# Fetching expert tiles by a plain transfer instead of a row-by-row gather, and a second weight copy on VectorE

## The chip, the core and the metric

The kernel runs on one core of a Trainium2 chip. The metric is device time in microseconds (us). The engines are named as in the profile: PE (TensorE, its weight loads apart as PEld), DVE (VectorE), ACT (ScalarE), POOL (GpSimd) and SP (SyncE, which here only issues transfers). The kernel before was timed three times: 283.83 us median, 283.54 to 286.17.

## The reference

The input passes through an attention block and then through a mixture of experts with one expert per token.

```
phi(x)  = outer product of (S1 x) and (S2 x), 8 x 8 = 64 features       x: 4 batches, 4 heads, 1088 rows, 32 wide
kv      = sum over rows of phi(k) v ;   z = sum over rows of phi(k)
attn    = phi(q) kv / (phi(q) z + 1e-6)                                  -> x: 4352 tokens x 128
logits  = x @ w_gate ;  expert = argmax ;  gate = softmax(logits)[expert]
out[t]  = gate * relu(x[t] @ w1[expert]) @ w2[expert]                    8 experts, w1 128 x 1024, w2 1024 x 128
```

All of it is in fp32.

## The kernel before

**Attention.** Tasks named T, P, V, E, B, U, N (transposes, projections, sums, queries) work on 512-row chunks of each batch. **Routing.** For each batch `b`, C.b chooses the expert, G.b takes the exponentials, R.b ranks the tokens within their experts, and S.b scatters the batch's rows into `xs_dram`, a DRAM table with 4352 places for each expert. A row is 130 words: 128 of x, the gate and the token number. S.b is 8 or 9 indirect transfers on POOL, one for each 128 tokens. So the rows of one expert stand one behind another.

**Tiles.** The expert part works on tiles of 128 rows of one expert: 34 fixed ones (`JMIN`) and up to 7 more, of which parts of 4, 2 and 1 are taken by three branches, as the routing needs them. Tiles 0 to 9 (`JE` is 10) hold rows of batches 0 and 1 alone and may begin before batches 2 and 3 are scattered; tile 10 and later ones wait for all. Two tables, made on VectorE by `table` (tasks W.0 to W.6, and later `piece`), say for each tile which expert it has (`woff`) and where its rows are.

**One tile.** `gather(j)` (task F.j) fetches the tile's rows from `xs_dram` into `xg_of(j)`; `x_in(j)` (I.j) transposes them on PE, copies the transpose on ACT, and lets VectorE copy the expert's w1 (128 x 1024) out of `w1_all` at a register's offset; `up(j)` (Y.j) is 8 matmuls into `ph` and a relu, on ACT for the early tiles and half on ACT, half on VectorE from tile 7 on; `rows_out(j)` makes the numbers of the output rows; `down(j)` (Z.j with `rows_out`) is 8 matmuls into `py` and the scaling by the gate on ACT; `store(j)` scatters the rows to `out` on POOL. In the profile each fp32 matmul stands as two records, so a tile has 16 records of `ph`, 16 of `py` and one transpose `xgTp`.

**Order.** Each engine runs its instructions in the order in which the program records them. ORDER, a list of task names, sets it up to tile 4's `down`; behind it a loop over the tiles takes over: in turn j it records x_in(j+2), rows_out(j), up(j+1), down(j), the gather of tile j+6 (from j = 6 on), a gather of one of the 7 possible extra tiles (`optional`) and the stores.

**What the change touches.** `gather` (L691) is an indirect transfer on POOL with one row number for each partition; `down` (L733) loads a register on PE and addresses `w2_all` with it, so each of its 8 matmuls has a register operation ahead of it; the loop at L842 says how many stores each turn records; `table` (L534) makes the row numbers `grow`.

Of the kernel before, what the change touches and what calls it, by code (L numbers as in the profile page):

```python
# [47 lines left out]
ORDER = """  # L50
finish_s T.K00 T.K01 P.K00 P.K01 T.K11 T.K10 T.kr0 V.K00 P.kr0 D P.K11 P.K10 T.Q00 T.Q01 L T.Q11
V.K01 P.Q01 E.0 P.Q00 B.0 P.Q11 T.qr0 U.Q01 U.Q00 T.K21 T.Q10 N.Q00 P.qr0 N.Q01 C.0 P.Q10 P.K21
V.K10 V.K11 T.kr1 G.0 T.K20 R.0 U.qr0 U.Q11 E.1 P.K20 B.1 A.2 U.Q10 T.Q20 N.qr0 N.Q10 N.Q11 V.K20
V.K21 C.1 P.Q20 P.kr1 G.1 T.K31 T.Q21 A.3 R.1 T.K30 W.0 U.Q20 P.Q21 P.K30 P.K31 E.2 W.1 T.Q30 W.2
T.Q31 T.qr1 W.3 U.Q21 S.0 P.Q31 B.2 W.4 P.Q30 V.K30 S.1 N.Q21 N.Q20 V.K31 P.qr1 W.5 F.0 W.6 E.3 C.2
U.Q30 B.3 F.1 F.2 U.qr1 U.Q31 F.3 N.qr1 F.4 N.Q30 G.2 I.0 F.5 N.Q31 I.1 R.2 Y.0 I.2 I.3 C.3 Y.1 Z.0
I.4 Y.2 Z.1 F.6 G.3 S.2a I.5 S.2b R.3 Y.3 Y.4 S.3a S.3b Z.2 F.7 Y.5 Z.3 F.8 Z.4 I.6 F.9
"""
# [3 lines left out]
def kernel(  # L62
# [111 lines left out]

    zeros = const.tile([128, 128], FP, name="zeros")
    nc.vector.memset(zeros, 0.0)
    idle = bank_ps("idle")
    for i in range(12):
        nc.tensor.matmul(idle[:, 0:128], lhsT=zeros, rhs=zeros, start=True, stop=True)  # L179

# [270 lines left out]

    xs_dram = dram.tile([E * NTOK, XW], I32, name="xs_dram")

    def route(b):
# [74 lines left out]


    tiles = {}
    done = const.tile([128, E], FP, name="done")

    def table(g, n, j0):  # L534
# [30 lines left out]
        if g:  # L565

            bits = const.tile([128, 3], I32, name="bits")
            nc.vector.tensor_scalar(bits[:, 0:1], cum[:, E - 1:E], float(JE - JMIN), None, ALU.add)
            begin = t1("begin", I32)
            for i, (run, below) in enumerate(((4, 0), (2, 4), (1, 6))):  # L570
                if i:
                    nc.vector.tensor_scalar(begin[:, i:i + 1], bits[:, 0:1], below, None, ALU.bitwise_and)
# [219 lines left out]
    for j in range(sum(name[0] == "Z" for name in begun), JMIN):  # L794
# [81 lines left out]
```

## Time and profile before

| | us |
|---|---|
| median of three runs | 283.83 |
| the profiled execution | 284.85 |
| its span, first to last instruction | 282.7 |
| PE busy | 231.8 (82% of the span) |
| DVE / ACT / POOL busy | 108.5 / 75.4 / 134.2 |
| transfers: gathers x41, scatters x34, stores x34 and x7 on POOL | mean 1.05, 1.07, 1.03 and 1.17 each |

A row of the page or of an answer gives an engine's busy time, the idle time ahead of a group and in `<-` what ended it. "issue" is idle time in which the engine waited for nothing that the profile shows. PEclk is TensorE's granted clock as a share of 2.4 GHz (0.5 is 1.2 GHz).

### The profile page before, as it was taken

Reading aid. Unit: us, or ns where it says so; the run is one execution under the profiler, and the core shown is the slowest. Engines: PE = TensorE matmul, PEld = TensorE weight load, DVE = VectorE, ACT = ScalarE, POOL = GpSimd, SP = SyncE. Lnnn points to the kernel's source line nnn. Section 1 sums busy time; section 2 is a strip of 40 time slices with the busy share of each in tenths; the row PEclk is TensorE's granted clock in tenths of the full one; section 3 lists DMA queues with packets and bytes.
Section 4 is the critical chain, followed back from the end, with each engine's and each line's share of the span. In section 5 each row is a group of like instructions: output and inputs, shape, how many; then the busy total and the mean of one; then the engine's idle time right before and its main releaser. Section 6 shows DMA issues by size and latency. Waiting matters only on the chain.

```text
span 282.7 us, 6720 instructions
## 1 busy us (share of the span) xinstructions
PE 231.8 (82%) x2558; PEld 216.2 (76%) x2558; DVE 108.5 (38%) x303; ACT 75.4 (27%) x198; POOL 134.2 (47%) x165
## 2 busy tenths in 40 slices
PE   8989875957975959669939559887887999999993
PEld 7989764836954949539939349787777998999993
DVE  4656735515844805410641012324323234224320
ACT  2555420404340305013200012221212232333321
POOL 5520373273072564740057747667576156263223
PEclk9999997975996886957977758999997999999999
DMA  6969999211011010110002111111110001010000
GB/s 196 286 191 361 367 377 376 84 47 31 2 40 28 30 48 20 59 38 0 2 21 56 36 38 33 50 35 44 33 48 26 17 21 44 14 37 21 20 9 21
DMA packets 23009, 22.69 MB, mean 80 GB/s; under 512 B 5844, under 2 KB 20184, under 8 KB 22976
## 3 DMA queue, kind: packets, MB, share of 16 engines
q1 hardware_dynamic: 18160, 14.95, 16.3%
q0 software_dynamic: 3712, 7.15, 8.6%
q8 instruction: 23, 0.38, 0.6%
q10 hardware_dynamic: 1104, 0.13, 0.3%
q14 instruction: 10, 0.08, 0.1%
HBM read 17.81 MB, written 4.95 MB: 81 GB/s over the span
## 4 chain that ended last, share of the span: by engine, by line
PE 65%; issue 19%; another core or an unknown queue 6%; ACT 3%; DMA 2%; POOL 2%; DVE 1%; POOLq 1%; ACTq 0%; DVEq 0%
PE ph L724 23%; PE py L740 18%; PE kv L342 4%; PE ab_K L319 4%; PE qp_Q L405 3%; PE nd_Q L417 3%; PE ab_Q L319 3%; PE idle L179 2%; PE tp_Q L310 1%; PE xgTp L703 1%; DMA out_dram<-y,to 1%; PE tp_K L310 1%; ACT q_pT_Q L408 1%; POOL out_dram L747 1%
## 5 line engine op out<-in xcount | busy, mean ns | idle before, releaser
L740 PE MATMUL py<-w_all,hT 128*128 x592 | 81.5, 290 | 9.9 <-issue 6.7
L724 PE MATMUL ph<-xgT,w 128*128 128x128 f32 x592 | 83.6, 295 | 7.3 <-issue 5.2
L724 PEld LDWEIGHTS ph<-xgT,w 128*128 128x128 f32 x592 | 77.7, 209 | 12.1 <-issue 9.9
L740 PEld LDWEIGHTS py<-w_all,hT 128*128 128x128 f32 x592 | 75.9, 205 | 12.8 <-issue 10.1
L692 POOL DMA_INDIRECT x_rows<-xs_dram,grow x41 | 42.9, 1047 | 48.4 <-issue 28.2
L731 DVE TENSOR_SCALAR hT<-ph 128x512 f32<-128x512 f32 x30 | 20.7, 691 | 101.6 <-ACT hT L726 70.0
L747 POOL DMA_INDIRECT out_dram<-y,to x34 | 35.0, 1031 | 43.3 <-ACT xgT L705 28.4
L515 POOL DMA_INDIRECT xs_dram<-x_rows,row_i x34 | 36.3, 1067 | 31.9 <-DVE base_e L509 9.5
L726 ACT ACTIVATE hT<-ph 128x512 f32<-128x512 f32 x37 | 22.2, 599 | 73.2 <-PE ph L724 36.9
L709 DVE COPY w<-w_all 128x1024 f32 x38 | 26.4, 704 | 20.7 <-remote 16.6
L743 ACT ACTIVATE y<-py,x_rows 128x128 f32<-128x128 f32 x34 | 12.5, 368 | 60.3 <-remote 27.6
L417 PE MATMUL nd_Q<-kvx,q_pT_Q 128*64 128x82 f32 x256 | 13.0, 244 | 7.0 <-issue 5.7
L703 PE MATMUL xgTp<-ident,x_rows 128*128 128x128 f32 x38 | 10.5, 298 | 7.8 <-DMA x_rows<-xs_dram,grow 4.4
L417 PEld LDWEIGHTS nd_Q<-kvx,q_pT_Q 128*64 128x64 f32 x256 | 10.8, 141 | 7.6 <-issue 5.6
L319 PE MATMUL ab_K<-s_cat,xT_K 128*64 128x64 f32 x256 | 12.0, 233 | 4.8 <-issue 4.4
L327 DVE TENSOR_TENSOR k_p<-half_K 128x1024 f32<-128x1024 f32 x8 | 10.5, 1328 | 11.7 <-issue 6.1
L319 PEld LDWEIGHTS ab_K<-s_cat,xT_K 128*64 128x64 f32 x256 | 9.7, 144 | 6.7 <-issue 6.3
L705 ACT COPY xgT<-xgTp 128x128 f32<-128x128 f32 x38 | 9.5, 265 | 15.3 <-remote 8.0
L327 DVE TENSOR_TENSOR q_p_Q<-half_Q 128x1024 f32<-128x1024 f32 x8 | 10.4, 1324 | 8.1 <-ACT half_Q L326 8.1
L342 PEld LDWEIGHTS kv<-k_p,v_aug 128*33 128x33 f32 x256 | 9.0, 125 | 4.1 <-issue 4.1
L342 PE MATMUL kv<-k_p,v_aug 128*33 128x64 f32 x256 | 10.4, 239 | 1.9 <-issue 1.9
L703 PEld LDWEIGHTS xgTp<-ident,x_rows 128*128 128x128 f32 x38 | 5.5, 149 | 7.5 <-issue 7.2
(164 smaller groups left out, 193.4 us busy)
## 6 DMA issues: line engine op xcount, KB each, us to landing
w_all<-in_moe_w_dram SPq DMA_DIRECT2D x16, 512.0 KB
k<-in_k_dram SPq DMA_DIRECT2D x4, 512.0 KB
v<-in_v_dram SPq DMA_DIRECT2D x4, 512.0 KB
q<-in_q_dram SPq DMA_DIRECT2D x4, 512.0 KB
x_rows<-xs_dram,grow POOLq DMA_INDIRECT x41
xs_dram<-x_rows,row_i POOLq DMA_INDIRECT x34
out_dram<-y,to POOLq DMA_INDIRECT x34
q_rem<-in_q_dram SPq DMA_DIRECT2D x4, 32.0 KB
```

The costliest lines, as they stand in the source:

```text
L319: nc.tensor.matmul(ab[ts(m, 64)].rearrange("p (g i r) -> p g i r", g=4, i=n)[:, :, i], lhsT=st["xT"][:, ds(i * 128 + m * 64, 64)], rhs=s_c ...
L327: nc.vector.tensor_tensor(f.rearrange("p g (a b) -> p g a b", a=R), half[:, :, 0:R, None].broadcast_to(shape), half[:, :, None, R:2 * R].b ...
L342: nc.tensor.matmul(kv[b][g * RR:g * RR + DA, ts(n, RR)], lhsT=v1[:, h], rhs=k_p[:, h], start=(first and n == 0), stop=last, skip_group_che ...
L417: nc.tensor.matmul(nd[ts(m, 64), i, ds(hp * 2 * KC, 2 * KC)], lhsT=t[:, ds((i * NP + hp) * 128 + m * 64, 64)], rhs=kvx[bs[m]][:, hp].rearr ...
L515: d = nc.gpsimd.indirect_dma_start(out=xs_dram[:], out_offset=bass.IndirectOffsetOnAxis(ap=row_i[:, u:u + 1], axis=0), in_=x[:, u, :].bitc ...
L692: d = nc.gpsimd.indirect_dma_start(out=xg_of(j).bitcast(I32), out_offset=None, in_=xs_dram[:], in_offset=bass.IndirectOffsetOnAxis(ap=tile ...
L709: nc.vector.tensor_copy(out=w1, in_=w1_all[:, ds(wo, F)])
L724: nc.tensor.matmul(ph[:, ts(c, 128)], lhsT=w1[:, ts(c, 128)], rhs=xT, start=True, stop=True)
L726: nc.scalar.activation(hT[:, 0:512], ph[:, 0:512], AF.Relu)
L731: nc.vector.tensor_scalar(hT[:, 512:1024], ph[:, 512:1024], 0.0, None, ALU.max)
L740: nc.tensor.matmul(py[:, :DM], lhsT=hT[:, ts(c, 128)], rhs=w2_all[:, ds(wo + c * DM, DM)], start=(c == 0), stop=(c == NFC - 1))
L747: d = nc.gpsimd.indirect_dma_start(out=out[:], out_offset=bass.IndirectOffsetOnAxis(ap=to_of(j), axis=0), in_=y, in_offset=None, bounds_ch ...
```

## The change

Rows come by one plain transfer. `xs_dram` is filled with zeros early, by one transfer on SP's queue between the loads (8 x 128 rows, from a zeroed tile). The tables give each tile's first row instead of 128 row numbers; for a tile that would run past its expert's rows, the first row moves back, and rows that belong to another tile get an output row number outside `out`. `gather` loads that first row into a register of SP and issues a plain 128 x 130 transfer on SP's queue. `up(j)` first copies the expert's w2 on VectorE at a register's offset into one of three buffers (`w2_of`), and `down(j)` reads it there with fixed addresses. Stores are recorded two for each turn of the loop. ORDER is another list.

```
 ORDER = """
-finish_s T.K00 T.K01 P.K00 P.K01 T.K11 T.K10 T.kr0 V.K00 P.kr0 D P.K11 P.K10 T.Q00 T.Q01 L T.Q11
+finish_s T.K00 T.K01 P.K00 P.K01 T.kr0 T.K11 T.K10 P.kr0 D V.K00 P.K10 P.K11 T.Q01 T.Q00 L T.Q11 V.K01 P.Q00
...
-I.4 Y.2 Z.1 F.6 G.3 S.2a I.5 S.2b R.3 Y.3 Y.4 S.3a S.3b Z.2 F.7 Y.5 Z.3 F.8 Z.4 I.6 F.9
+N.Q31 I.1 F.4 R.2 F.5 S.2a Y.0 I.2 S.2b F.6 F.7 N.qr1 C.3 I.3 Y.1 G.3 Z.0 Y.2 I.4 Y.3 Z.1 Y.4 R.3 F.8 Z.2
+S.3a I.5 Z.3 Z.4 W.6 S.3b Y.5 F.9 I.6
...
+    xs_dram = dram.tile([E * NTOK, XW], I32, name="xs_dram")
+    zeros = const.tile([128, XW], FP, name="zeros")
+    nc.vector.memset(zeros, 0.0)
...
     load_rem(lambda b: q_rem[:, b // 2], q, nc.sync, 0)
+    nc.sync.dma_start(out=xs_dram.rearrange("(e r) c -> r e c", e=E)[0:128],
+                      in_=zeros[:, None, :].bitcast(I32).broadcast_to([128, E, XW]))
     load_main("k", k, 2)
...
-        nc.vector.tensor_scalar(loc, loc, 128.0, iota_p, ALU.mult, ALU.add)
+        nc.vector.tensor_scalar(loc, loc, 128.0, None, ALU.mult)
...
+            nc.vector.scalar_tensor_tensor(begin, of, -128.0, loc, ALU.add, ALU.min)
+            nc.vector.tensor_scalar(begin, begin, 0.0, None, ALU.max)
+            nc.vector.scalar_tensor_tensor(first, ej, float(NTOK), begin, ALU.mult, ALU.add)
...
+    def w2_of(j):
+        if not w2_own:
+            w2_own.append([att.tile([128, JC * H, RR], FP, tag="k_p", name=f"w2_0_{i}", bufs=3)
+                           .rearrange("p g f -> p (g f)") for i in range(3)])
+            w2_own.append([])
+        if j >= JMIN and not w2_own[1]:
+            w2_own[1].extend(att.tile([128, F], FP, tag="q_pT", name=f"w2_1_{i}", bufs=3) for i in range(3))
+        return w2_own[j >= JMIN][j % 3]
...
     def gather(j):
-        d = nc.gpsimd.indirect_dma_start(
-            out=xg_of(j).bitcast(I32), out_offset=None, in_=xs_dram[:],
-            in_offset=bass.IndirectOffsetOnAxis(ap=tiles[j][1], axis=0),
-            bounds_check=E * NTOK - 1, oob_is_err=False)
+        _, (row,) = nc.values_load_multi_w_load_instructions(
+            tiles[j][1], engines=[mybir.EngineType.SP], min_val=0, max_val=E * NTOK - 128,
+            skip_runtime_bounds_check_because="the table keeps a tile within its expert's rows")
+        d = nc.sync.dma_start(out=xg_of(j).bitcast(I32), in_=xs_dram[ds(row, 128), :])
...
     def up(j):
         xT, w1 = xT_of(j), w1_of(j)
+        _, (wo,) = nc.values_load_multi_w_load_instructions(
+            tiles[j][0], engines=[DVE], min_val=0, max_val=(E - 1) * F,
+            skip_runtime_bounds_check_because="the table clamps the expert to the last one")
+        nc.vector.tensor_copy(out=w2_of(j), in_=w2_all[:, ds(wo, F)])
...
     def down(j):
-        hT = hT_of(j)
-        _, (wo,) = nc.values_load_multi_w_load_instructions(
-            tiles[j][0], engines=[PE], min_val=0, max_val=(E - 1) * F,
-            skip_runtime_bounds_check_because="the table clamps the expert to the last one")
+        hT, w2 = hT_of(j), w2_of(j)
...
-            nc.tensor.matmul(py[:, :DM], lhsT=hT[:, ts(c, 128)], rhs=w2_all[:, ds(wo + c * DM, DM)],
+            nc.tensor.matmul(py[:, :DM], lhsT=hT[:, ts(c, 128)], rhs=w2[:, ts(c, DM)],
...
-        for _ in range(0 if j < 6 else j % 2 if optional else 2 if j + 1 < JMIN else JT):
+        for _ in range(2 if j + 1 < JMIN else JT):
```

The order on POOL, from the last batch's scatter on; `x_rows` stands for the gathered rows, `out_dram` for the output. Before:

```order
L515 DMA xs_dram<-x_rows_201,row_i_1660 34816x130 x9
L692 DMA x_rows_193<-xs_dram,grow_1314 128x130
L692 DMA x_rows_195<-xs_dram,grow_1314 128x130 x2
L692 DMA x_rows_193<-xs_dram,grow_1870 128x130 x4
L692 DMA x_rows_195<-xs_dram,grow_1870 128x130
L747 DMA out_dram<-y_1571,to_0_1542 4352x128
L692 DMA x_rows_193<-xs_dram,grow_1870 128x130
L692 DMA x_rows_195<-xs_dram,grow_1870 128x130
```

With the change:

```order
L517 DMA xs_dram<-x_rows_195,row_i_754 34816x130 x8
L517 DMA xs_dram<-x_rows_197,row_i_999 34816x130 x9
L517 DMA xs_dram<-x_rows_201,row_i_1476 34816x130 x8
L517 DMA xs_dram<-x_rows_203,row_i_1699 34816x130 x9
L769 DMA out_dram<-y_1615,to_0_1589 4352x128
L769 DMA out_dram<-y_1615,to_1_1590 4352x128
L769 DMA out_dram<-y_1615,to_2_1591 4352x128
```

All gathers have left POOL: the four scatters stand behind one another, and the stores follow at once.

The order on SP, behind the last load of the experts' matrices (`w_all`), where before nothing but the end of the program stood. With the change:

```order
L713 TENSOR_LOAD first_row_1294
L716 ISA
L716 DMA x_rows_195<-xs_dram 128x130
L713 TENSOR_LOAD first_row_1294
L716 ISA
L716 DMA x_rows_195<-xs_dram 128x130
```

Each gather is now a register load, an address operation and one transfer, and these three are repeated for every tile.

The order on VectorE for one of the late tiles: `w` and `w_0_1` are the copies' targets, `to` the output rows, `hT` the relu's half. Before:

```order
L706 TENSOR_LOAD woff_1831
L709 ISA
L709 COPY w_0_1431<-w_all 128x1024
L718 TENSOR_TENSOR to_13_1555<-x_rows_193,inv_i_1890 128x1
L731 TENSOR_SCALAR hT_2_1502<-ph_2176 128x512
```

With the change:

```order
L727 TENSOR_LOAD woff_1861
L730 ISA
L730 COPY w_0_1418<-w_all 128x1024
L739 TENSOR_TENSOR to_13_1603<-x_rows_195,inv_i_1933 128x1
L743 TENSOR_LOAD woff_1861
L746 ISA
L746 COPY w_0_2_1500<-w_all 128x1024
L756 TENSOR_SCALAR hT_2_1513<-ph_2263 128x512
```

A second register load and a second 128 x 1024 copy now stand ahead of the relu of the same turn.

## Rows read from the trace of the kernel before

**Rows 1.** The page's chain that ended last: share of the span by engine.

```profile
PE 65%; issue 19%; another core or an unknown queue 6%; ACT 3%; DMA 2%; POOL 2%; DVE 1%; POOLq 1%; ACTq 0%; DVEq 0%
```

**Rows 2.** Busy time by stretch: each engine's us (instructions), PEclk, DMA share, GB/s.

```profile
20.00:30.00 10.00, 9.98 (x246) 9.41 (x243) 7.46 (x18) 4.62 (x11) 0.60 (x1) 1.00 0.99 334
78.30:90.70 12.40, 7.25 (x97) 5.52 (x94) 4.79 (x19) 3.30 (x10) 7.01 (x7) 0.84 0.15 39
90.70:109.00 18.30, 15.28 (x109) 14.70 (x110) 8.93 (x32) 4.67 (x13) 8.34 (x8) 0.78 0.09 30
109.00:129.40 20.40, 14.68 (x86) 12.66 (x85) 6.31 (x27) 4.49 (x11) 12.13 (x12) 0.75 0.13 40
145.70:216.90 71.20, 57.63 (x400) 53.82 (x401) 18.35 (x44) 13.21 (x37) 48.59 (x47) 0.84 0.14 40
216.90:278.40 61.50, 60.77 (x543) 60.39 (x541) 19.98 (x43) 17.89 (x48) 24.38 (x23) 1.00 0.08 23
```

**Rows 3.** Groups by line, PE: the first of 145.7:216.9, the others of 216.9:278.4.

```profile
L724 PE MATMUL ph<-xgT,w 128*128 128x128 f32 x193 | 30.5, 302 | 6.6 <-issue 5.2 <-ACT xgT L705 0.8
...
L740 PE MATMUL py<-w_all,hT 128*128 x273 | 33.4, 275 | 0.7 <-ACT y L743 0.7
L724 PE MATMUL ph<-xgT,w 128*128 128x128 f32 x256 | 31.2, 275 | 0.0
```

**Rows 4.** Timeline of PE, steady: start us, us, operation, count [idle before <-releaser].

```profile
261.78 0.27 PE L703 MATMUL xgTp<-ident,x_rows 128*128 128x128 f32 x1
...
265.46 0.27 PE L703 MATMUL xgTp<-ident,x_rows 128*128 128x128 f32 x1
```

**Rows 5.** Timeline of PE from the first late tile on.

```profile
145.76 0.45 PE L703 MATMUL xgTp<-ident,x_rows 128*128 128x128 f32 x1 [4.37 <-DMA x_rows<-xs_dram,grow]
146.00 3.63 PE L724 MATMUL ph<-xgT,w 128*128 128x128 f32 x16
149.43 2.99 PE L740 MATMUL py<-w_all,hT 128*128 x16
...
165.11 1.80 PE L724 MATMUL ph<-xgT,w 128*128 128x128 f32 x4 [0.84 <-issue]
...
195.54 0.30 PE L703 MATMUL xgTp<-ident,x_rows 128*128 128x128 f32 x1 [1.81 <-DMA out_dram<-y,to]
```

**Rows 6.** Timeline of POOL: first and last of 18 transfers in a row.

```profile
142.97 1.11 POOL L692 DMA_INDIRECT x_rows<-xs_dram,grow  x1 [18.47 <-issue]
...
165.41 0.99 POOL L692 DMA_INDIRECT x_rows<-xs_dram,grow  x1 [0.30 <-issue]
```

**Rows 7.** Timeline of PE about the first tile.

```profile
81.44 1.36 PE L417 MATMUL nd_Q<-kvx,q_pT_Q 128*64 128x82 f32 x32 [0.73 <-ACT q_pT_Q L408]
...
82.99 0.60 PE L417 MATMUL nd_Q<-kvx,q_pT_Q 128*64 128x82 f32 x7
...
88.39 1.10 PE L417 MATMUL nd_Q<-kvx,q_pT_Q 128*64 128x82 f32 x12 [0.89 <-issue]
...
90.73 3.37 PE L724 MATMUL ph<-xgT,w 128*128 128x128 f32 x16 [0.52 <-DVE den_Q L422]
```

**Rows 8.** The page's groups: busy us, mean ns of one | idle before, releaser.

```profile
L747 POOL DMA_INDIRECT out_dram<-y,to x34 | 35.0, 1031 | 43.3 <-ACT xgT L705 28.4
...
L709 DVE COPY w<-w_all 128x1024 f32 x38 | 26.4, 704 | 20.7 <-remote 16.6
```

**Rows 9.** Timeline of VectorE: two of the w1 copies.

```profile
109.58 0.92 DVE L709 COPY w<-w_all 128x1024 f32 x1 [0.42 <-PE ph L724]
...
142.52 0.69 DVE L709 COPY w<-w_all 128x1024 f32 x1 [0.29 <-issue]
```

**Rows 10.** Timeline of SP's queue: the longest and the last issue of a load.

```profile
22.64 3.80 SPq L150 DMA_DIRECT2D w_all<-in_moe_w_dram  x1
...
44.95 0.43 SPq L151 DMA_DIRECT2D w_all<-in_moe_w_dram  x1
```

**Rows 11.** The chain of waits in order of time: a late gather until it landed.

```profile
142.97 2.65 DMA x_rows<-xs_dram,grow
```

More of the change, by code (lines that the diff above doesn't have):

```diff
@@ L50 @@
 ORDER = """
-finish_s T.K00 T.K01 P.K00 P.K01 T.K11 T.K10 T.kr0 V.K00 P.kr0 D P.K11 P.K10 T.Q00 T.Q01 L T.Q11
[L52 to L56, printed above, removed]
-I.4 Y.2 Z.1 F.6 G.3 S.2a I.5 S.2b R.3 Y.3 Y.4 S.3a S.3b Z.2 F.7 Y.5 Z.3 F.8 Z.4 I.6 F.9
+finish_s T.K00 T.K01 P.K00 P.K01 T.kr0 T.K11 T.K10 P.kr0 D V.K00 P.K10 P.K11 T.Q01 T.Q00 L T.Q11 V.K01 P.Q00
+E.0 P.Q01 B.0 P.Q11 T.qr0 U.Q00 U.Q01 T.Q10 T.K21 N.Q00 P.qr0 P.Q10 N.Q01 V.K10 C.0 P.K21 G.0 V.K11 U.Q10
+T.K20 T.kr1 R.0 U.Q11 E.1 P.K20 U.qr0 B.1 T.Q20 N.qr0 A.3 N.Q11 N.Q10 C.1 A.2 P.Q20 P.kr1 G.1 V.K20 T.K31
+S.0 T.K30 T.Q21 R.1 W.0 V.K21 U.Q20 P.K31 E.2 P.Q21 W.1 P.K30 B.2 T.Q31 W.2 S.1 W.3 T.Q30 U.Q21 T.qr1 N.Q20
+N.Q21 V.K30 P.qr1 W.4 P.Q30 V.K31 W.5 P.Q31 F.0 E.3 U.qr1 U.Q30 B.3 F.1 F.2 F.3 C.2 G.2 U.Q31 N.Q30 I.0
+N.Q31 I.1 F.4 R.2 F.5 S.2a Y.0 I.2 S.2b F.6 F.7 N.qr1 C.3 I.3 Y.1 G.3 Z.0 Y.2 I.4 Y.3 Z.1 Y.4 R.3 F.8 Z.2
+S.3a I.5 Z.3 Z.4 W.6 S.3b Y.5 F.9 I.6
 """
@@ L172 @@
     load_main("q", q, 2)
-    zeros = const.tile([128, 128], FP, name="zeros")
-    nc.vector.memset(zeros, 0.0)
     idle = bank_ps("idle")
     for i in range(12):
-        nc.tensor.matmul(idle[:, 0:128], lhsT=zeros, rhs=zeros, start=True, stop=True)
+        nc.tensor.matmul(idle[:, 0:128], lhsT=zeros[:, 0:128], rhs=zeros[:, 0:128], start=True, stop=True)
     ident = const.tile([128, 128], FP, name="ident")
@@ L449, in query_rem @@
               lambda: rows_of(2 * r + 1, J, 1))
-    xs_dram = dram.tile([E * NTOK, XW], I32, name="xs_dram")
     def route(b):
@@ L526, in route @@
         task[f"S.{b}a"], task[f"S.{b}b"] = lambda: scatter(range(J // 2 + n - J)), lambda: scatter(range(J // 2 + n - J, n))
+    parts = [range(JMIN, JMIN + 4), range(JMIN + 4, JMIN + 6), range(JMIN + 6, JMIN + 7)]
     tiles = {}
@@ L569, in table @@
             begin = t1("begin", I32)
-            for i, (run, below) in enumerate(((4, 0), (2, 4), (1, 6))):
-                if i:
-                    nc.vector.tensor_scalar(begin[:, i:i + 1], bits[:, 0:1], below, None, ALU.bitwise_and)
+            nc.vector.memset(begin[:, 0:1], 0)
+            for i, below in (1, 4), (2, 6):
+                nc.vector.tensor_scalar(begin[:, i:i + 1], bits[:, 0:1], below, None, ALU.bitwise_and)
             for i in (2, 1, 0):
@@ L577, in table @@
             begin_f = t1("begin_f")
-            nc.vector.tensor_copy(out=begin_f[:, 1:3], in_=begin[:, 1:3])
+            nc.vector.tensor_scalar(begin_f[:, 0:3], bits, 0, float(JT), ALU.is_equal, ALU.mult)
+            nc.vector.tensor_tensor(begin_f[:, 0:3], begin_f[:, 0:3], begin[:, 0:3], ALU.add)
             jn = tj("jn")
-            nc.vector.tensor_copy(out=jn, in_=jio[:, 0:n])
             base = JMIN - JE
-            nc.vector.tensor_scalar(jn[:, base + 4:base + 6], jio[:, base:base + 2], begin_f[:, 1:2], None, ALU.add)
-            nc.vector.tensor_scalar(jn[:, base + 6:base + 7], jio[:, base:base + 1], begin_f[:, 2:3], None, ALU.add)
+            nc.vector.tensor_copy(out=jn[:, 0:base], in_=jio[:, 0:base])
+            for i, tiles_here in enumerate(parts):
+                a, m = tiles_here[0] - JE, len(tiles_here)
+                nc.vector.tensor_scalar(jn[:, a:a + m], jio[:, base:base + m], begin_f[:, i:i + 1], None, ALU.add)
             yield
@@ L601, in table @@
         yield
-        gr = tj("grow", I32, const)
-        iv = None
+        first, iv = tj("first_row", I32, const), None
         if g:
@@ L622, in table @@
             nc.vector.tensor_scalar(of, of, cnt[:, 0:1], None, ALU.add)
-            inv = tj("inv")
-            nc.vector.tensor_tensor(inv, loc, of, ALU.is_ge)
+            begin = tj("begin_row")
+            nc.vector.scalar_tensor_tensor(begin, of, -128.0, loc, ALU.add, ALU.min)
+            nc.vector.tensor_scalar(begin, begin, 0.0, None, ALU.max)
+            nc.vector.scalar_tensor_tensor(first, ej, float(NTOK), begin, ALU.mult, ALU.add)
+            nc.vector.tensor_scalar(begin, begin, iota_p, None, ALU.add)
+            nc.vector.tensor_tensor(loc, begin, loc, ALU.is_lt)
+            nc.vector.tensor_tensor(begin, begin, of, ALU.is_ge)
+            nc.vector.tensor_tensor(loc, loc, begin, ALU.max)
             iv = tj("inv_i", I32, const)
-            nc.vector.tensor_scalar(iv, inv, float(2 ** 30), None, ALU.mult)
-            nc.vector.scalar_tensor_tensor(loc, ej, float(NTOK), loc, ALU.mult, ALU.add)
-            nc.vector.scalar_tensor_tensor(gr, inv, float(2 ** 22), loc, ALU.mult, ALU.add)
+            nc.vector.tensor_scalar(iv, loc, float(2 ** 30), None, ALU.mult)
         else:
-            nc.vector.scalar_tensor_tensor(gr, ej, float(NTOK), loc, ALU.mult, ALU.add)
+            nc.vector.scalar_tensor_tensor(first, ej, float(NTOK), loc, ALU.mult, ALU.add)
         for j in range(n):
-            tiles[j0 + j] = (wo[0:1, j:j + 1], gr[:, j:j + 1], None if iv is None else iv[:, j:j + 1])
+            tiles[j0 + j] = (wo[0:1, j:j + 1], first[0:1, j:j + 1], None if iv is None else iv[:, j:j + 1])
         if not g:
@@ L640, in table @@
             nc.vector.tensor_tensor(done, nt, before, ALU.min)
-    parts = [range(JMIN, JMIN + 4), range(JMIN + 4, JMIN + 6), range(JMIN + 6, JMIN + 7)]
     after = {16: 0, 20: 1, 24: 2}
@@ L676 @@
     w1_of = buffers("w1", (3, 2), None, tags=(("k", 3), ("q", 3)))
+    w2_own = []
+    def w2_of(j):
[6 more added lines that the diff above has]
+        return w2_own[j >= JMIN][j % 3]
     hT_of = buffers("hT", (3, 2), None, tags=(("v", 3), ("v_aug", 2)))
```

## The prediction

> **What bounds the kernel now.** I read the chain that ended last first, then busy time by stretch, then the timelines of PE, POOL and VectorE in the stretches that stood out.
>
> The chain lies on PE for 65% of the span, and 19% of it is "issue": PE has work, and no wait that the profile shows holds it [rows 1]. The stretches say where. From 216.9 us to the end PE is busy 60.77 of 61.5 us [rows 2], and one tile follows another in 265.46 - 261.78 = 3.68 us [rows 4]. This is the kernel's best pace, with PE the bound. The stretch ahead of it has 193 `ph` records, which at 16 a tile is 12 tiles [rows 3], and takes 71.2 us [rows 2]. At 3.68 us these tiles are 44.2 us of work. So 27.0 us are lost there.
>
> What loses them? POOL works without a break at the start of that stretch: 18 transfers from 142.97 to 165.41, 0.30 us apart [rows 6]. While they run, PE's matmuls come in single steps with "issue" gaps, as 4 records in 1.80 us behind a gap of 0.84 [rows 5], and the granted clock of the stretch is 0.84 where it is 1.00 afterwards [rows 2]. The same picture stands elsewhere. At the first tile, beside 7 gathers in a row, 32 records of `nd_Q` take from 82.99 to 89.49 = 6.50 us, and the 32 just ahead of them 1.36 [rows 7]. Beside the scatters too: the stretch at 109 has 86 PE records in 20.40 us at clock 0.75, with 12 POOL transfers [rows 2]. A steady tile has 33 records in 3.68 us, so those 86 are about 9.6 us of work and 10.8 are lost. By the same rate the stretch at 90.7 loses 6.1 (109 records, 12.2 us of work, 18.30 taken; 8 POOL transfers) [rows 2]. After 216.9, with 23 POOL transfers in 61.5 us instead of 47 in 71.2, there is no loss [rows 2]. Why PE starves beside a row of POOL transfers no row says. That it does stands in each of these stretches.
>
> **The change part by part.** The sum starts from the profiled execution's 284.85 us, its span of 282.7 and 2.15 around it. It is 1.02 above the median of 283.83.
>
> *Gathers leave POOL in the late stretch.* Of POOL's 47 transfers there only the stores remain, one for each tile or two in a turn, and no long row of them. I take PE at its pace of 3.68. Two parts of the 27.0 stay. The first is the slow clock after the wait for the second table: `ph` and `py` of the first late tile take from 146.00 to 152.42, 6.4 us instead of 3.68, so 2.7 more [rows 5]. The second is the idle time of 1.8 us ahead of tile 18's transpose, the first one behind the first branch [rows 5]. So 27.0 - 2.7 - 1.8 = **22.5 us gained**. The ends: nothing, if PE starves for another reason; 27, if those two parts go as well. I take the value nearest to the undisturbed stretch, because it has the same work with sparse POOL transfers.
>
> *Gathers leave POOL at the first tile.* The `nd_Q` records return to 1.36 from 6.50 us, 5.1; and the first `ph` meets a full clock, 3.37 against half a steady tile, 1.84, which is 1.5 [rows 4, 7]. **6.6 us gained**, between 0 and 6.6.
>
> *Scatters stay* with their losses of 6.1 and 10.8 us. Behind the last one, 3 gathers leave POOL, but stores of up to five tiles stand ready in their place: the row of transfers is as long as before. **0**, between 2 us lost and 10.8 gained.
>
> *SP's part of a gather.* A register load, an address operation and an issue. A load on VectorE shows 0.29 us ahead of the copy that needs it [rows 9], and SP's issues take 0.43 to 3.80 us [rows 10]. The last load of weights was issued at 45 us [rows 10], long before the first gather at 78, so nothing is queued ahead. What waits on SP holds up only later gathers, which are recorded six tiles ahead. The gather at 142.97 landed after 2.65 us [rows 11]; at 0.29 + 0.43 of SP and a landing like that, the first late tile arrives about as before and PE's wait of 4.37 us stays [rows 5]. **0**, between 1 gained and 3 lost; that a gather costs 3.80 each time is a rival below.
>
> *The w2 copies.* One more copy for each of 37 tiles, 0.69 us with a load of 0.29 ahead [rows 9]. In the steady stretch VectorE is busy 19.98 us for 16 tiles, 1.25 a tile [rows 2]; with 0.98 more it is 2.2 of 3.68, so PE covers it. If that cover went, each tile would be late by what exceeds 3.68. At the first tile VectorE also has two batches' routing, and `py` of tile 0 waits for its copy: **1.0 us lost**, between 0 and 3.
>
> *Register operations leave PE.* In the steady stretch a record of `py`, which has them, takes 275 ns, and one of `ph`, which has none, 275 as well [rows 3]: **0**, hidden by the matmuls already in PE's queue. If that cover went there would be a gain and no loss.
>
> *Zero fill and the new list.* The fill writes 8 x 128 rows of 520 bytes, 0.53 MB. At the 334 GB/s of the stretch at 20 us, when transfers were at 0.99 of their share and PE still busy 9.98 of 10 [rows 2], this is 1.6 us of transfers, hidden as those were: 0, up to 1.6 lost. The list of tasks keeps the same attention work; I see no term in it and allow 2 us either way. The table's few changed operations on small tiles are inside that.
>
> Sum: 22.5 + 6.6 - 1.0 = 28.1; 284.85 - 28.1 = 256.8, less 1.02 for the median's scale, **256 us**.
>
> **A rule against it.** Copies and POOL's transfers meet on VectorE: of 38 copies the mean is 0.704, a free one 0.69, one beside a scatter 0.92 [rows 8, 9]. So the meeting costs a copy at most 0.23 us here, and I take no more. The Trainium skill, SBUF — State Buffer, section Who interferes with whom, says that a VectorE copy in two-port mode and GpSimd exclude each other, and that the later one waits for the whole of the other's instruction. By that rule a copy would wait a full 1.03 us transfer; the trace so far agrees in kind and not in size.
>
> **The rivals.**
> - *The scatters hurt less* (15%). With 3 transfers fewer behind the last scatter, and with tiles that come earlier, the loss of 10.8 in the stretch at 109 goes. For it: it stands with the longest row but one. Against: the stores take the gathers' place. 256 - 10.8 = 245 us.
> - *Copies wait for POOL* (6%). Six w2 copies stand in the early tiles, where the scatters run, and each waits a whole transfer of 1.03 us [rows 8]: 256 + 6 = 262. Against: 0.92 is the longest that I found there. This is the rule above at full size.
> - *PE starves from the fetches themselves*, whichever queue they come from. Then 29 us stay lost and the copy is added: 284 + 1 = 285, no change (8%); or half of it stays, 256 + 14.5 = 270 (9%). For it: the rows are fetched as 128 pieces either way, and no row names the cause. Against: at 20 us SP's transfers fill the queues at 0.99 and PE is busy 9.98 of 10 [rows 2]. This rival is also the one that the change doesn't do what it is said to: the gathers move and the gaps stay.
> - *Slower: SP becomes the bound* (5%). If SP issues a gather only when the last has landed, and the issue takes the longest that is seen, a tile costs 0.29 + 3.80 + 2.65 = 6.7 us [rows 9, 10, 11], 3.0 more than PE needs, and 27 late tiles lose 83: 339 us. It decides from 3.68 + 28/27 = 4.7 us a gather on; above it the change is slower than before. Against: the longest issue is from a stretch with full queues, a free one takes 0.43.
>
> **How the numbers follow.** The forecast, 256 with 250 to 262 for its own terms' bounds, has 57%. The range goes down to the rival at 245 and a little below, **243**, and up to the half case, **270**; outside are the cases of 285 and 339 and the tails, under 20%. A measurement of this kernel tells about 1% from no change, 281 to 287 here. Faster: forecast, 245, 262 and 270, 87%. Same: 8%. Slower: 5%.
>
> **What would show it.** Right: no "issue" gaps in PE after the table's wait, a tile each 3.68 us from the first late one on, and `ph` of tile 0 some 6 us earlier. The scatters' gaps are still there, with stores of five tiles right behind them. SP's issues under 1 us; each w2 copy at 0.69 and its matmuls never waiting for VectorE after the first tiles. Wrong: gaps in PE beside SP's gathers; transposes that wait for a gather later than the first late one; a scatter stretch of another length.

## The result, and the profile after

The kernel after takes 263.34 us (median of 4 runs, 260.93 to 266.77), the kernel before beside it 284.64 (283.54 to 286.17): a ratio of 0.922, 95% interval 0.913 to 0.931. The profiled execution of after is its fastest run, 260.93 us, with a span of 259.2.

Where the time came from is told by four moments in the two traces (before in [rows 4, 5, 7] and the rest of those timelines):

| us | before | after | gained since the row above |
|---|---|---|---|
| end of tile 0's `ph` | 94.10 | 87.66 | 6.44 |
| first late tile's transpose | 145.76 | 142.92 | -3.60 |
| end of the last `py` | 278.35 | 250.50 | 25.01 |
| end of the span | 282.7 | 259.2 | -4.35 |

The chain of waits is at 2% "issue", where it was at 19% [rows 1]; what it could follow is less than half of the span.

```profile
PE 37%; issue 2%; POOL 1%; DVE 1%; DMA 1%; another core or an unknown queue 1%; POOLq 1%; ACT 0%; SPq 0%; ACTq 0%
```

The stretches of [rows 2] again, after (each engine's busy us and its records, PEclk, DMA share, GB/s):

```profile
78.30:90.70 12.40, 11.60 (x175) 10.18 (x172) 10.05 (x31) 5.84 (x17) 1.41 (x2) 1.00 0.26 60
90.70:109.00 18.30, 16.31 (x134) 15.65 (x133) 10.29 (x34) 5.81 (x14) 9.61 (x10) 0.91 0.11 36
109.00:129.40 20.40, 5.48 (x39) 5.25 (x38) 6.95 (x31) 2.15 (x6) 11.27 (x12) 0.68 0.11 39
145.70:216.90 71.20, 70.91 (x627) 70.54 (x626) 38.50 (x81) 21.48 (x58) 25.09 (x22) 0.99 0.16 42
```

The late stretch has 627 PE records where it had 400, at a clock of 0.99 instead of 0.84. The stretch at 109 has become worse: 39 records instead of 86. PE's timeline shows both, and the first tile (to be read with [rows 5, 7]):

```profile
81.96 1.36 PE L421 MATMUL nd_Q<-kvx,q_pT_Q 128*64 128x82 f32 x32
...
83.52 1.36 PE L421 MATMUL nd_Q<-kvx,q_pT_Q 128*64 128x82 f32 x32
...
85.64 2.02 PE L749 MATMUL ph<-xgT,w 128*128 128x128 f32 x16 [0.29 <-DVE den_Q L426]
...
110.02 1.95 PE L749 MATMUL ph<-xgT,w 128*128 128x128 f32 x16
111.81 0.38 PE L724 MATMUL xgTp<-ident,x_rows 128*128 128x128 f32 x2
127.10 3.46 PE L749 MATMUL ph<-xgT,w 128*128 128x128 f32 x16 [14.92 <-ACT xgT L726]
...
142.92 0.30 PE L724 MATMUL xgTp<-ident,x_rows 128*128 128x128 f32 x1 [3.20 <-DMA x_rows<-xs_dram]
143.06 3.11 PE L749 MATMUL ph<-xgT,w 128*128 128x128 f32 x16
145.96 2.52 PE L762 MATMUL py<-w,hT 128*128 128x128 f32 x16
148.32 0.27 PE L724 MATMUL xgTp<-ident,x_rows 128*128 128x128 f32 x1
...
152.00 0.27 PE L724 MATMUL xgTp<-ident,x_rows 128*128 128x128 f32 x1
...
246.76 3.74 PE L762 MATMUL py<-w,hT 128*128 128x128 f32 x32
```

The last `py` of before stands in its timeline of PE as:

```profile
274.61 3.74 PE L740 MATMUL py<-w_all,hT 128*128 x32
```

`nd_Q` has no gaps any more, and behind the first late tile a tile follows each 3.68 us, as from 148.32 to 152.00; only one comes later than that by more than 0.2 us, by 0.9 at 189.85, behind six stores in a row on POOL. But PE's records stop for 14.92 us at 112. PE waits for ACT, and ACT's timeline says that ACT waits too:

```profile
110.02 0.37 ACT L765 ACTIVATE y<-py,x_rows 128x128 f32<-128x128 f32 x1 [2.96 <-remote]
118.66 0.37 ACT L765 ACTIVATE y<-py,x_rows 128x128 f32<-128x128 f32 x1 [8.27 <-remote]
125.81 0.60 ACT L751 ACTIVATE hT<-ph 128x512 f32<-128x512 f32 x1 [6.78 <-remote]
```

"remote" stands where the profile names no releaser; with one core, none is elsewhere. The `y` at 118.66 needs the `py` whose records end at 110.2, the `hT` at 125.81 the `ph` whose records end at 112.0: in the trace PE's semaphore goes up at 110.00, 118.64 and 125.72 and not in between, so PE's results reach ACT 8 and 14 us behind their records (whose ends the profile models). POOL's timeline in that stretch is one row of 14 transfers, the last 9 scatters and 5 stores. One of PE's results comes through in the middle of it, the next 2 us behind its end at 123.6:

```profile
105.83 0.97 POOL L517 DMA_INDIRECT xs_dram<-x_rows,row_i  x1 [6.25 <-DVE to L737]
107.11 0.97 POOL L517 DMA_INDIRECT xs_dram<-x_rows,row_i  x1 [0.30 <-issue]
...
117.53 0.97 POOL L769 DMA_INDIRECT out_dram<-y,to  x1 [0.30 <-issue]
...
122.64 0.97 POOL L769 DMA_INDIRECT out_dram<-y,to  x1 [0.30 <-issue]
```

Late instructions do not explain it: among the DMA records of this trace, a packet of the kind "instruction" starts at 106.78 and takes 0.96 us, and the next one starts at 136.82.

The end of the span is later against the last `py` than before: 8.70 us instead of 4.35. SP's waits (waiting line, what it waits for, us in total, times, longest) name a wait at the program's end, before first, then after:

```profile
SPq L871 <- PEq L871: 0.7, 2, 0.5
```

```profile
SPq L892 <- PEq L892: 5.0, 2, 4.5
```

The copies on VectorE, w1 (L730) and w2 (L746), against 0.704 of [rows 8]:

```profile
L730 DVE COPY w<-w_all 128x1024 f32 x38 | 26.0, 693 | 12.4 <-remote 10.6
L746 DVE COPY w<-w_all 128x1024 f32 x37 | 25.6, 693 | 6.4 <-PE py L762 5.2
```

### The profile page after: what moved, and what is told of

Read it like the earlier page. It is cut to its first block, busy times and chain, and to the rows that moved or that the text cites. A ratio compares the mean times of both kernels' runs of the same rounds, so it can differ in the third digit from the quotient of the medians.

```text
span 259.2 us, 6683 instructions
## 1 busy us (share of the span) xinstructions
PE 214.7 (83%) x2558; PEld 206.2 (80%) x2558; DVE 130.7 (50%) x347; ACT 76.1 (29%) x198; POOL 91.0 (35%) x124
## 5 line engine op out<-in xcount | busy, mean ns | idle before, releaser
L749 PE MATMUL ph<-xgT,w 128*128 128x128 f32 x592 | 75.9, 283 | 15.9 <-ACT xgT L726 14.9
L749 PEld LDWEIGHTS ph<-xgT,w 128*128 128x128 f32 x592 | 72.0, 198 | 16.8 <-ACT xgT L726 15.5
L762 PE MATMUL py<-w,hT 128*128 128x128 f32 x592 | 74.1, 279 | 2.0 <-issue 1.7
L762 PEld LDWEIGHTS py<-w,hT 128*128 128x128 f32 x592 | 70.8, 195 | 2.6 <-issue 2.2
L769 POOL DMA_INDIRECT out_dram<-y,to x34 | 37.0, 1089 | 88.1 <-ACT xgT L726 67.7
L517 POOL DMA_INDIRECT xs_dram<-x_rows,row_i x34 | 35.3, 1038 | 48.9 <-DVE base_e L511 24.7
L730 DVE COPY w<-w_all 128x1024 f32 x38 | 26.0, 693 | 12.4 <-remote 10.6
L746 DVE COPY w<-w_all 128x1024 f32 x37 | 25.6, 693 | 6.4 <-PE py L762 5.2
L323 PE MATMUL ab_Q<-s_cat,xT_Q 128*64 128x64 f32 x256 | 11.9, 238 | 5.6 <-issue 5.6
L323 PEld LDWEIGHTS ab_Q<-s_cat,xT_Q 128*64 128x64 f32 x256 | 10.3, 151 | 6.6 <-issue 6.6
L215 POOL COPY v_aug<-v 128x1024 f32<-128x1024 f32 x4 | 4.8, 1208 | 15.9 <-DMA v<-in_v_dram 15.9
```

Source lines behind the costliest of these rows:

```text
L323: nc.tensor.matmul(ab[ts(m, 64)].rearrange("p (g i r) -> p g i r", g=4, i=n)[:, :, i], lhsT=st["xT"][:, ds(i * 128 + m * 64, 64)], rhs=s_c ...
L517: d = nc.gpsimd.indirect_dma_start(out=xs_dram[:], out_offset=bass.IndirectOffsetOnAxis(ap=row_i[:, u:u + 1], axis=0), in_=x[:, u, :].bitc ...
L730: nc.vector.tensor_copy(out=w1, in_=w1_all[:, ds(wo, F)])
L746: nc.vector.tensor_copy(out=w2_of(j), in_=w2_all[:, ds(wo, F)])
L749: nc.tensor.matmul(ph[:, ts(c, 128)], lhsT=w1[:, ts(c, 128)], rhs=xT, start=True, stop=True)
L762: nc.tensor.matmul(py[:, :DM], lhsT=hT[:, ts(c, 128)], rhs=w2[:, ts(c, DM)], start=(c == 0), stop=(c == NFC - 1))
```

## The experiments

The theory: a long row of GpSimd's indirect transfers, one straight behind the other, holds TensorE until the row ends; the change won by breaking such rows up, and lost where one is left. Each kernel was timed in three rounds beside the kernel before (282.5 to 286.5 us there). Kernels that are the same up to tile 0's `ph` reach it between 85.6 and 91.7 us in their profiles, so stretches are compared from that `ph` on. In after, 173.6 us lie from it to the end, in the profile of its fastest run; in e1 and e3, whose edits moved nothing (see below), 177.2 and 176.1. Differences below 4 us from after show nothing by themselves.

**The gathers alone put back** (e4).

```diff
+        nc.vector.tensor_scalar(gr, first, iota_p, None, ALU.add)
-        d = nc.sync.dma_start(out=xg_of(j).bitcast(I32), in_=xs_dram[ds(row, 128), :])
+        d = nc.gpsimd.indirect_dma_start(out=xg_of(j).bitcast(I32), out_offset=None, in_=xs_dram[:],
+            in_offset=bass.IndirectOffsetOnAxis(ap=tiles[j][1], axis=0), ...)
```

> Only the gathers are put back: an indirect transfer on GpSimd's queue by 128 row numbers (first row plus the partition's number), instead of SP's plain one. The copies of the second matrix, the stores' pace and the list of tasks stay as in the changed kernel. By the prediction's terms the time rises by 22.5 for the late stretch and 6.6 for the first tile: 285 to 292 us. Rival: the gain came from the other edits (the copies, the list, the stores' pace): 263 to 270 us.

Measured: 288.21 us (285.28 to 288.93), ratio to before 1.015 [1.007, 1.024]. The whole gain hangs on the gathers. From the first late transpose to the last `py` it takes 20.3 us longer than after, of the 25.0 that this stretch had gained. Its late stretch is like that of before again:

```profile
145.70:216.90 71.20, 55.37 (x414) 52.46 (x413) 32.58 (x81) 13.76 (x38) 46.56 (x43) 0.89 0.14 37
```

Its wait at the end is short, too, so the 4.4 us there go with SP's fetches; whether with the register or with the transfers, no run separates:

```profile
SPq L894 <- PEq L894: 0.7, 2, 0.5
```

**The w2 copies alone undone** (e9).

```diff
...
-        nc.vector.tensor_copy(out=w2_of(j), in_=w2_all[:, ds(wo, F)])          # in up(j)
...
-                             rhs=w2[:, ts(c, DM)],                             # in down(j)
+                             rhs=w2_all[:, ds(wo + c * DM, DM)],               # wo: a register of PE
```

> Only the copy of the second matrix is undone: TensorE reads w2 at a register's offset again, and the 37 copies of 0.69 us leave VectorE. The gathers stay on SP's queue. By the prediction's terms (copies 1.0 lost, register operations 0) the time is that of the changed kernel or 1 us less: 262 to 264 us. Rival: the register operations held TensorE, and the copies are part of the gain: 267 us or more, with 'issue' gaps or a tile longer than 3.68 us. Rival: the copies cost more than 1 us at the start of the tiles, where VectorE also has the routing: 258 to 260 us.

Measured: 267.4 us (265.85 to 268.94), ratio 0.932 [0.925, 0.939]; after has 0.922 [0.913, 0.931], and the intervals touch. The 262 to 264 that I expected did not come, and the rival's 267 did. The profile says somewhat more: from the first late transpose to the end it takes 119.8 us against 116.3, and has "issue" gaps of 1.92, 0.65 and 1.09 us there, the first behind a branch, as in [rows 5], the other two beside six stores in a row:

```profile
180.57 0.30 PE L724 MATMUL xgTp<-ident,x_rows 128*128 128x128 f32 x1 [1.92 <-issue]
```

So no cost of the copies is seen, and they are rather worth 2 to 3 us (e1 and e3 take 117.3 and 117.4 us there); the time alone doesn't prove it.

**The stores held back** (e1), **or in rows** (e3).

```diff
-        for _ in range(2 if j + 1 < JMIN else JT):
+        for _ in range(0 if j < 9 else 2 if j + 1 < JMIN else JT):    # e1
+        n_out = 2 if j + 1 < JMIN else JT                             # e3
+        if 8 < j < 26:
+            n_out = len(waiting) if len(waiting) >= 9 else 0
+        for _ in range(n_out):
```

> The stores of the first tiles are held until tile 9 has been computed, so the row of GpSimd transfers that begins with the last scatters (9 scatters and then 5 stores, 14 in all) is 9 long. Theory 'row': TensorE is held while a long row of indirect transfers runs, and is let go when the row ends; the idle time of 14.9 us ahead of tile 6's ph shrinks by the 5 transfers at 1.28 us, 6.4 us, and the kernel takes about 257 us. Rival 'count': every transfer costs TensorE the same wherever it stands, so the held stores cost it later: 263 us, within 1%. Rival 'other': the idle time has to do with the table or the scatters' landing: 263 us and the 14.9 us stay.

> Between tiles 9 and 25 the stores are not issued as they come but in rows of at least 9, one straight behind the other; their number and bytes stay. In that stretch TensorE now has no idle time. Theory 'row': each of the two or three rows of 9 to 12 transfers (12 to 15 us) holds TensorE for 4 to 9 us and brings its clock down: 8 to 25 us slower, 271 to 288 us. Rival 'count' and rival 'only the scatters or the gathers do it': 263 us, within 1%, and TensorE's tiles stay at 3.68 us.

Measured: 262.41 us (260.94 to 267.85) and 264.03 (259.6 to 264.4), both as after. They tell nothing of the theory, because the edits moved nothing that counts: in e1, too, the five stores stand straight behind the scatters. POOL's own list has no other work there, so a store that is recorded later runs at the same moment, when its `y` is ready. In e3 the stores that should have stood in a row come one by one:

```profile
151.97 0.96 POOL L769 DMA_INDIRECT out_dram<-y,to  x1 [5.82 <-ACT xgT L726]
155.66 1.06 POOL L769 DMA_INDIRECT out_dram<-y,to  x1 [2.72 <-ACT xgT L726]
```

**Real rows of stores** (e8).

```diff
-                store(waiting.pop(0))                                 # as e3, and
+                store(waiting.pop(-1 if 8 < j < 26 else 0))
```

> The rows of stores again, now with the newest tile's store first, so that the row really waits for it and the others stand ready behind it (in the earlier try the stores ran as soon as each tile was ready, since nothing in GpSimd's own list stood ahead of them, and the edit moved nothing there). Two rows of 13 and 10 stores in the late stretch, no gather and no scatter, the same number of transfers and bytes. Theory 'row of indirect transfers': each row holds TensorE: 8 to 20 us slower than the changed kernel, 271 to 283 us. Rival 'count': 263 us, within 1%. Rival 'fetches or scatters to the staging rows only': 263 us.

Measured: 280.88 us (279.93 to 282.26), ratio 0.989 [0.978, 0.999], as the theory said. The same transfers, in rows, cost 17.5 of the 21.3 us that the change had gained. The first row has 13 stores; its first and last, and PE:

```profile
183.18 1.06 POOL L769 DMA_INDIRECT out_dram<-x_rows,to  x1 [32.48 <-ACT xgT L726]
...
199.20 0.97 POOL L769 DMA_INDIRECT out_dram<-y,to  x1 [0.30 <-issue]
```

```profile
191.99 0.57 PE L749 MATMUL ph<-xgT,w 128*128 128x128 f32 x3 [0.45 <-issue]
200.38 3.78 PE L762 MATMUL py<-w,hT 128*128 128x128 f32 x16 [7.82 <-issue]
```

PE goes on beside the first six transfers, then nearly stops, and starts again as the row ends, at half its pace (3.78 us for 16 records, 1.95 in a steady tile). By the steady 3.68 us a tile, this row of 13 cost 11.4 us, and the second one, of 11 stores, 5.5.

**Eleven fetches more, in three ways** (e5, e6, e7), behind tile 14's store; `ids` holds 0 to 127.

```diff
+        if j == 14:
+            for i in range(11):
+                nc.gpsimd.indirect_dma_start(out=extra[:, i], in_=xs_dram[:],              # e5
+                    in_offset=bass.IndirectOffsetOnAxis(ap=ids, axis=0), ...)
+                nc.gpsimd.dma_start(out=extra[:, i], in_=xs_dram[0:128, :])                # e6
+                nc.sync.dma_start(out=extra[:, i], in_=xs_dram[0:128, :])                  # e7
```

> Behind tile 14's store 11 more fetches of 128 rows of 520 bytes stand in a row on GpSimd's queue, indirect by row numbers 0 to 127, into a buffer that nothing reads. All else is the changed kernel; in this stretch its TensorE has no gaps. Theory 'row of indirect transfers': while they run one behind the other, 1.28 us each, 14 us, TensorE shows 'issue' gaps or late signals and a lower clock: 4 to 12 us slower than the changed kernel, 267 to 275 us. Rival 'scatters only' (it is the rows written to DRAM that hold TensorE): 263 us, within 1%.

> The same 11 extra fetches on GpSimd's queue, plain instead of indirect (rows 0 to 127 by one address). Theory 'row of indirect transfers': what hurts is GpSimd's work row by row; plain ones leave TensorE alone: 263 us, within 1%. Rival 'GpSimd's queue': any transfer that GpSimd issues hurts: 267 to 275 us, as with the indirect ones. Rival 'fetches': 267 to 275 us here and from SP too.

> The same 11 extra plain fetches in a row, but on SP's queue. Theory 'row of indirect transfers' and rival 'GpSimd's queue': 263 us, within 1%, TensorE's tiles stay at 3.68 us. Rival 'fetches' (128 pieces of 520 bytes, whichever queue they come from, starve TensorE): 267 to 275 us.

Measured: indirect 280.58 us (277.65 to 282.25), ratio 0.983 [0.965, 1.001]; plain on GpSimd's queue 269.93 (268.72 to 271.56), 0.949 [0.940, 0.957]; plain on SP's 268.64 (267.47 to 270.14), 0.944 [0.936, 0.953]. The indirect ones cost more than the 267 to 275 that the theory gave. From tile 0's `ph` to the end: 189.6, 178.6 and 176.7 us (after: 173.6). The indirect ones run from 178.63 to 193.06, with a store straight ahead of them and one behind; by the steady rate this row of 13 cost 13.3 us. PE beside it:

```profile
183.96 0.27 PE L727 MATMUL xgTp<-ident,x_rows 128*128 128x128 f32 x1
184.07 1.07 PE L752 MATMUL ph<-xgT,w 128*128 128x128 f32 x6
...
187.51 1.13 PE L752 MATMUL ph<-xgT,w 128*128 128x128 f32 x5 [0.82 <-issue]
...
196.62 3.78 PE L765 MATMUL py<-w,hT 128*128 128x128 f32 x16 [7.05 <-ACT y L768]
```

Plain ones from POOL, all 11 issued within 6.25 us, with PE beside them:

```profile
180.34 6.25 POOL L869 DMA_DIRECT2D extra<-xs_dram  x11
```

```profile
182.30 0.27 PE L725 MATMUL xgTp<-ident,x_rows 128*128 128x128 f32 x1
...
185.98 0.27 PE L725 MATMUL xgTp<-ident,x_rows 128*128 128x128 f32 x1
...
189.66 0.27 PE L725 MATMUL xgTp<-ident,x_rows 128*128 128x128 f32 x1
```

3.68 us a tile: nothing is lost. That their row takes only 6.25 us is not the reason. In e5 ACT's `y`, which needs the `py` whose records end at 180.44, came 2 us late when the indirect row had run for 3.8 us:

```profile
182.45 0.37 ACT L768 ACTIVATE y<-py,x_rows 128x128 f32<-128x128 f32 x1 [3.10 <-PE ph L752]
```

Nor is it the packets: the DMA records of e5 and e6 hold the same numbers of packets of each size, and their pages of the profile give 2752 packets of 5.23 MB in the queue "software_dynamic" for both (after: 2400 of 4.50 MB).

Nothing is lost beside SP's 11 either, from 165.31 to 170.96, with transposes at 164.33, 168.01 and 171.69. The times of e6 and e7 lie where the rivals were put, though, and that is not their transfers' doing. Both reach tile 0's `ph` 5.5 and 6.0 us later than after did, and lose 2.6 and 1.5 more up to the first late transpose (e1: 2.6), all of it before an extra transfer is issued; why the tiles begin later in them, no run shows. In e6, 1.8 us more are gaps at 195.7 to 197.7, beside a row of indirect stores that the extra work had put together. So what holds PE are indirect transfers, and neither GpSimd's queue nor the fetches. What it is about an indirect transfer, no run tells.

**The last 9 scatters spaced** (e2), **all 34** (e10), **all with a shorter pause** (e11).

```diff
+    scratch = const.tile([128, 512], FP, name="scratch")
...
+                if b in (3,):                                  # e10, e11: range(4)
+                    for _ in range(2):                         # e11: range(1)
+                        nc.gpsimd.memset(scratch, 0.0)
```

> Two GpSimd memsets of 128x512 f32 (about 1.1 us together) behind each of the 9 last scatters; the number of transfers stays 14, but the scatters are no row any more and the last of them is about 10 us later. Theory 'row': TensorE's idle time of 14.9 us falls below 7 (only the stores behind are still a row of 5), tiles 6 to 9 are computed earlier, and the late tiles start at about the same time or some us earlier than now: 255 to 263 us. Rival 'count': the same loss is spread over a longer time: 263 to 266 us with the same TensorE loss. Rival 'busy': it is GpSimd being at work, not its transfers, that holds TensorE; then the idle time grows by the 10 us of memsets: 270 us or more.

> Two memsets of 128x512 f32 (1.13 us) behind every one of the 34 scatters, not only behind the last 9. Theory 'row of indirect transfers': the gaps beside the other three rows of scatters go too (about 3, 6 to 10 and 3 us of 'issue' in the profiles so far), less 1 to 3 us because the third row ends later and the fourth starts behind it: 242 to 249 us. Rival: those gaps are in places where TensorE has time, and the loads set the end there: 250 to 254 us, as with the last row alone.

> The same with one memset (0.57 us) behind each scatter, so a transfer each 1.85 us instead of 2.4 (the row as it was: 1.28). If this is spacing enough, the last scatter ends about 5 us earlier than with two, and TensorE's wait for the first late tile shrinks by as much: 3 to 5 us faster than with two memsets. Rival: what clears the way needs more than half a transfer's time; TensorE's gaps come back in part beside each row: slower than with two memsets, 248 to 260 us.

Measured: e2 252.34 us (249.13 to 257.59), ratio 0.884 [0.876, 0.892]; e10 255.3 (252.41 to 256.63), 0.893 [0.887, 0.899]; e11 234.33 (232.77 to 235.11), 0.819 [0.814, 0.824]. e2 is faster than its 255 to 263. Its scatters come each 2.3 to 3.1 us, and the wait of 14.92 us is 1.18:

```profile
108.90 0.97 POOL L518 DMA_INDIRECT xs_dram<-x_rows,row_i  x1 [7.82 <-DVE to L741]
109.86 1.13 POOL L523 MEMSET scratch<- 128x512 f32 x2
111.22 0.97 POOL L518 DMA_INDIRECT xs_dram<-x_rows,row_i  x1 [0.23 <-issue]
```

```profile
116.87 2.05 PE L753 MATMUL ph<-xgT,w 128*128 128x128 f32 x16 [1.18 <-ACT xgT L730]
...
133.84 0.45 PE L728 MATMUL xgTp<-ident,x_rows 128*128 128x128 f32 x1 [5.76 <-DMA x_rows<-xs_dram]
```

The price stands in the second line: the late tiles wait for the last scatter. In e10 that price is paid twice, and it eats the gain. PE waits for rows at the first tile and at the first late one:

```profile
79.25 0.47 PE L728 MATMUL xgTp<-ident,x_rows 128*128 128x128 f32 x1 [11.34 <-DMA x_rows<-xs_dram]
...
132.16 0.45 PE L728 MATMUL xgTp<-ident,x_rows 128*128 128x128 f32 x1 [13.63 <-DMA x_rows<-xs_dram]
```

So e10 missed its 242 to 249, and its rival's 250 to 254 too: the 1 to 3 us that I had set off for later rows were far too few. With one memset, a transfer each 1.7 to 2.4 us, the rows are thin enough and early enough; I had expected 3 to 5 us from the shorter pause, and it gave 21, since of the two waits for rows the first is gone and the second is 4.00 us. e11's stretches, to be read with those of after above:

```profile
78.30:90.70 12.40, 11.89 (x113) 11.64 (x112) 11.71 (x25) 5.03 (x12) 11.40 (x13) 1.00 0.16 45
90.70:109.00 18.30, 17.12 (x153) 16.89 (x153) 16.79 (x53) 6.35 (x17) 16.65 (x21) 1.00 0.12 38
109.00:129.40 20.40, 15.94 (x128) 15.69 (x127) 12.32 (x34) 3.89 (x11) 12.48 (x13) 0.92 0.30 79
```

**The kernel before, with pauses and nothing else** (e12): one memset behind each of its scatters and gathers.

```diff
+                nc.gpsimd.memset(scratch, 0.0)                 # behind each scatter
+        nc.gpsimd.memset(scratch, 0.0)                         # in gather(j), behind the transfer
```

> The kernel before, with nothing of the change (gathers indirect on GpSimd's queue, w2 by registers, its own list), and one memset of 128x512 f32 (0.57 us) behind each of the 34 scatters and 41 gathers, none behind the stores. GpSimd has about 43 us more to do. Theory 'row of indirect transfers': the change won because it thinned GpSimd's rows; thinning them by pauses wins too: TensorE's 'issue' gaps (19% of the chain before) go for the most part, and with 1.85 us a gather and 1.28 a store GpSimd keeps up with a tile each 3.68: 245 to 265 us. Rival: the gathers have to leave GpSimd, and more work there only delays them: 280 to 295 us.

Measured: 252.69 us (250.16 to 255.56), the kernel before beside it 284.41 (282.58 to 284.9). More work on POOL, and 32 us faster; faster than the change, too. The late stretch has as many indirect gathers and stores as ever, POOL is busy 60.15 us of 71.2 instead of 48.59 [rows 2], and PE does 613 records instead of 400:

```profile
145.70:216.90 71.20, 69.24 (x613) 68.56 (x612) 28.40 (x59) 20.11 (x54) 60.15 (x64) 1.00 0.14 39
```

What it still lacks is early rows, since its gathers stand behind the scatters on POOL's list:

```profile
112.48 0.45 PE L706 MATMUL xgTp<-ident,x_rows 128*128 128x128 f32 x1 [17.50 <-DMA x_rows<-xs_dram,grow]
```

## Why the prediction was right, and where it was off

It said 256 us, 243 to 270; 263.34 came. The profile's own sum was 284.85 - 28.1 = 256.8, and the profiled run took 260.93: 4.1 us more. The rest of the 7.3 is scale: the profiled run is 2.4 below the median of after, and the median of before came out 0.8 above the one that the forecast was put to. 263.34 lies above the 250 to 262 of the forecast's own terms. It is inside the range because that reaches up to the rival in which half of the gaps stay, and this is not what came. The terms' errors also cancelled in part: against the forecast, the late stretch and the copies were 2.5 and 1.0 us better, and the first tile, the scatters' stretch and the end 0.2, 3.6 and 4.35 worse.

- *Gathers leave POOL in the late stretch*: 22.5 forecast, 25.0 measured. Right, and e4, which gives 20.3 of it back, shows that the gathers do most of it. Of what I let stay, the 1.8 us behind the branch went as well; e9, where they are back, points to PE's registers. The slow clock at the first late tile stayed: 5.42 us for `ph` and `py`, against 6.4 forecast.
- *Gathers leave POOL at the first tile*: 6.6 forecast, 6.44 measured.
- *Scatters stay*: **the term that was mis-sized.** I took 0, between 2 lost and 10.8 gained, because the row of the last scatters was to stay as long. From tile 0's `ph` to the first late tile 3.60 us were lost. The row did stay, but with 14 transfers instead of 12, since five stores took the place of three gathers; the mechanism is the one that I had, and the loss beside it is no fixed sum. At the steady rate the stretch at 109 did 39 x 3.68 / 33 = 4.3 us of work in 20.4, so it lost 16.1 instead of 10.8; the one at 90.7 did 14.9 and lost 3.4 instead of 6.1. I took the losses of before over as if they were prices of the row. A scatter stretch of another length was one of my signs of being wrong, and it came.
- *SP's part*: the fetch itself was right, the first late one landed after 1.82 us, and PE's wait was 3.20 (2.65 and 4.37 in [rows 11, 5]). **Missing was the end:** 4.35 us, which no row of before could show, since SP fetched no tile there.
- *Copies*: 1.0 lost forecast; no cost is seen, and e9 is no faster without the w2 copies. All 75 copies have a mean of 0.693 us.
- *Zero fill, list and register operations*: no loss is seen; tile 0 begins as forecast. The registers' 0 was too low by the branch's gap, if e9 is read rightly.

Of the rivals, the fetches are refuted by e6 and e7, SP as the bound by the steady 3.68. "The scatters hurt less" had the right place: it did not happen by itself, but e2, 11.0 us faster than after, shows that the place was worth as much as the 10.8 us that I priced it at.

On the meeting of copies and POOL: the longest copy in after took 0.836 us, against 0.69 free, so the rival's 262 is near the measured time by chance. Where POOL had memsets between its transfers (e11), copies went up to 1.40 and memsets from 0.538 to 0.992. The Trainium skill, SBUF — State Buffer, section Who interferes with whom, has the one block for the whole of the other's instruction; the 0.7 us more beside memsets are of that size, the 0.15 beside transfers alone are not. The same section says that DMA never contends with a compute engine and that PE waits on no one. Were that all, e5 and e8 would have been as fast as after; they show PE standing still for 7.05 and 7.82 us beside rows of indirect transfers. That section is about SBUF's ports, and whether PE is held at a port, no run shows.

## What to carry to other kernels

Where PE shows "issue" gaps, late results or a falling clock, lay GpSimd's timeline beside it and count the indirect transfers that stand straight behind one another; in this kernel a row of 6 cost 0.9 us, rows of 8 cost 3.4 (after) and 6.1 (before), rows of 11 to 13 from 5.5 to 13.3 (e8, e5), and one of 14 cost 16.1. A pause of half a transfer between them, or a plain transfer on another queue, gave most of that time back here, as long as nobody waited for the last one of the row. And an instruction that is recorded later runs later only if its own engine's list has something ahead of it.

## What the runs showed that I had not expected

- PE's records can end long before its results are signalled: 8 and 14 us in after. A wait that is put down to "remote" was here a wait for PE, held.
- Giving an engine off the critical path 34 memsets of 0.59 us on the mean more to do made the kernel 29 us faster (263.34 to 234.33), and 75 of them made the kernel before 32 us faster.
- With the fetches on SP, by a register, the program's end is longer: SP's longest wait there is 4.5 us in after and in e9, and 0.5 in before and in e4. Why, no run shows.
- What stays open: what in an indirect transfer holds PE, and why it takes some transfers of a row (two to eight in these traces) before it begins.
